# Half of wq's odd rows and all of gate_w moved to GpSimd's DMA queue in a decode kernel

## The chip, the cores and the metric

The kernel runs on one core of one Trainium2 chip. The metric is the device time of one execution in microseconds. Before the change it is 1295.29 us, the median of 3 runs (1294.97 to 1295.49).

## What is computed

A decode step for 8 sequences mixes two branches of the same input x of 8 x 576: attention over a cache of 4096 keys and values for each of 32 heads, and a layer-normed feed-forward block. A sigmoid gate, one number per sequence, weighs the two.

```python
B, Sq, D = 8, 1, 576
H, Sk, Dh = 32, 4096, 128            # all tensors bf16
q = (x @ wq)                         # 576 x 4096, one query per head
scores = einsum("bhqd,bhkd->bhqk", q, k_cache) * (Dh ** -0.5)
p = softmax(scores)
a = einsum("bhqk,bhkd->bhqd", p, v_cache) @ wo
h = gelu(einsum("bsd,df->bsf", layernorm(x), w1) + b1)
b = einsum("bsf,fd->bsd", h, w2) + b2
g = sigmoid((x * gate_w).sum(-1, keepdims=True))
out = g * a + (1 - g) * b
```

The two caches are 268 MB each; every byte of them is read once.

## The kernel before, in words

The work on the caches is cut into 32 groups `n`: one sequence and 8 heads each, with 8 MiB of K and 8 MiB of V. A group's K lies in `KR` with 128 partitions (8 heads x 16 stretches of the keys) and 256 keys of 128 numbers in each. VectorE multiplies K by the query in eight pieces (`mult`, L500), TensorE adds the products up in PSUM with an identity as weights (L511, L183), and VectorE reduces the rest (L523). Softmax follows on VectorE and ScalarE (`softmax`, L540 to L556), then the product with V on TensorE (`pv`, L564), whose result goes to `OT_sb`. After the last group TensorE multiplies `OT_sb` by wo (`a_proj`, L754).

The order of work is written out by hand, one list of operations per engine (`Stream.op`), and each engine runs its list in order. TensorE's and VectorE's lists are loops over the groups. Waits are on semaphores: an operation names those that it needs, a DMA has one of its own. An engine that waits holds up all that stands behind it in its list, DMA issues included.

Nearly all loads are issued by SyncE, in this order: wq, the first K tile in two halves, w1, w2 (`load_w2`, which waits for the Q projection because `VB` holds wq until then), the second K tile (`load_k`, L328, which waits until VectorE is through with the first), the first V tile in two parts (`load_v`, L339; the second part waits for the feed-forward block, whose w2 lies there), and then K and V in turn, each as soon as its buffer is free. After the last V tile come the pieces of wo. ScalarE issues four small loads at the start: x, gate_w (repeated for 8 partitions), b1 and b2. GpSimd issues no DMA before the change; it sets constants at the start and does some elementwise work.

The part that is changed is the start. wq has 576 rows of 4096. Rows 0 to 511 lie in `wq_sb`, four per partition, so that four matmuls of 128 rows each cover them. The other 64 rows, here called the odd rows, come as 128 half rows (`halves`, `wq_t`), one per partition. To match, `spread` writes the odd 64 columns of x twice into a zeroed tile `xz`, once at the even places and once at the odd ones, and `transposed` (L424) turns x and `xz` into `xT_sb`, with six columns blocks of 8. A matmul over all 128 partitions with block 4 then uses the first halves of the odd rows, one with block 5 the second halves. The Q projection (L451) is 40 matmuls: 2 halves of the heads, 4 groups, 5 blocks. ScalarE copies the result (L454), TensorE spreads it over partitions (`q_of`, L465), ScalarE copies it to `q_bc` (L469) and to `q_n` (L475), and VectorE's first product (L500) can start.

The gate's sum is one fused multiply and reduce on VectorE (`t_gs`, L407), its sigmoid one ScalarE activation with a table load (`a_g`, L410). The feed-forward block's transposes of the normalised x use the same `up_ps` bank from column `YT_COL` on.

Of the kernel before, what the change touches and what calls it, by code (L numbers as in the profile page):

```python
# [144 lines left out]
def bass_gated_mix__mha_block_cached__mixer_channel_mlp__decode_kernel(  # L145
# [71 lines left out]
    junk = early([B, D])  # L217
    xz = early([B, 2, 64, 2])
    yz = early([B, 2, 64, 2])
    xT_sb = early([128, NKF + 2, B])  # L220
    yT_sb = sb("yT_sb", [128, NKF + 2, B], BF16)
# [57 lines left out]
    up_bank = (qb_ps, *tr_ps)  # L279
    YT_COL = 64  # L280

# [4 lines left out]
    def load(engine, dst, src, name, waits=()):  # L286
        return op(engine, lambda e: e.dma_start(dst, src), waits, dma=(nc.alloc_semaphore(name), 16))  # L287
# [85 lines left out]
    c_mA = memset("gpsimd", mA[:], 0.0)  # L373
    c_shift = memset("gpsimd", shift[:], 0.0)
    zeros = bass.AP(tensor=mA, offset=1, ap=[[pstride(mA), 128], [0, 512]])

    def blank(ps):
# [28 lines left out]
                                                   op0=ALU.add), [t])  # L406
    t_gs = op("vector", lambda e: e.tensor_tensor_reduce(out=junk, in0=x_sb, in1=gw8, scale=1.0, scalar=0.0,  # L407
                                                         op0=ALU.mult, op1=ALU.add, accum_out=stat[:, 8:9]), [ld_gw, t1])
    a_sqrt = aside("scalar", lambda e: e.activation(out=stat[:, 5:6], in_=stat[:, 4:5], func=ACT.Sqrt), [t_vpe])
    a_g = aside("scalar", lambda e: e.activation(out=stat[:, 9:10], in_=stat[:, 8:9], func=ACT.Sigmoid), [t_gs])  # L410
    G_COL, OMG_COL = 9, 10


    def spread(dst, src, waits):

        aside("scalar", lambda e: e.activation(out=dst[:, 0, :, 0], in_=src[:, 512:576], func=ACT.Copy), [*waits, c_z])
        return aside("scalar", lambda e: e.activation(out=dst[:, 1, :, 1], in_=src[:, 512:576], func=ACT.Copy))

    def transposed(src, srcz, col, waits):
        last = None  # L420
        for kt in range(NKF + 2):
            o = up_ps[:, col + kt * B:col + (kt + 1) * B]
            i = src[:, kt:NKF * 128:NKF] if kt < NKF else srcz[:, kt - NKF, :, :].rearrange("b r s -> b (r s)")
# [4 lines left out]
    def untransposed(dst, col, waits):  # L428
        return op("vector", lambda e: e.tensor_copy(
            out=dst.rearrange("p k b -> p (k b)"), in_=up_ps[:, col:col + (NKF + 2) * B]), waits)  # L430

    v_xz = spread(xz, x_sb, [ld_x])
    p_xT = transposed(x_sb, xz, 0, [ld_x, c_id, v_xz])
    v_xT = untransposed(xT_sb, 0, [p_xT])
# [4 lines left out]
    p_yT = transposed(y_sb, yz, YT_COL, [v_yz, v_xT])  # L439
    v_yT = untransposed(yT_sb[:, :, :], YT_COL, [p_yT])  # L440

    a_Q = []
    p_Q = None
    for half in range(2):
        for h in range(4):
            for kt in range(NKT):
                o = tr_ps[half][32 * h:32 * h + B, :]
                at = (kt * SK + half * (SK // 2) if kt < NKF else NKF * SK) + h * DH
                r = bass.AP(tensor=VB, offset=at, ap=[[pstride(VB), 128], [4 * DH, 4], [1, DH]])
                xi = kt if kt < NKF else NKF + half  # L450
                p_Q = aside("tensor", lambda e, o=o, r=r, kt=kt, xi=xi: e.matmul(  # L451
                    o, lhsT=xT_sb[:, xi, :], rhs=r, start=(kt == 0), stop=(kt == NKT - 1)),
                    [v_xT, *ld_wq, *c_ps] if h == kt == half == 0 else ())
        a_Q.append(aside("scalar", lambda e, half=half: e.activation(  # L454
            out=Q4[:, half * 512:(half + 1) * 512], in_=tr_ps[half][:, :], func=ACT.Copy, scale=inv_sqrt_dh), [p_Q]))
# [443 lines left out]
```

## Time and profile before

| | |
|---|---|
| median of 3 runs | 1295.29 us (1294.97 to 1295.49) |
| profiled execution, span of its instructions | 1293.1 us |
| around the span, by the median | 2.2 us |
| busy: TensorE / VectorE / ScalarE / GpSimd | 731.3 / 851.9 / 73.2 / 12.7 us |
| read from memory | 556.95 MB |

The span runs from the first to the last instruction of the profiled execution, and no time of its own is given for that execution outside of it; the 2.2 us are the median of the three runs less the span. Times in the views are microseconds from the start of the span. PE is TensorE, PEld its weight loads, DVE VectorE, ACT ScalarE, POOL GpSimd, SP SyncE; a `q` behind a name is the engine's sequencer, which issues DMAs. `L451` is line 451 of the kernel before. In rows in order of time the columns are start, duration, engine, line, operation, output and input, count, and in brackets the idle time ahead of it with what ended it. In rows by window the columns are the stretch, its length, busy time and count of each engine, the granted TensorE clock, the busy share of the 16 DMA engines and GB/s. In rows on DMA issues the last number is the time from issue to landing; in rows on queues the numbers are packets, MB and the share of 16 DMA engines' time.

### The profile page before, as it was taken

Reading aid. Unit: us, or ns where it says so; the run is one execution under the profiler, and the core shown is the slowest. Engines: PE = TensorE matmul, PEld = TensorE weight load, DVE = VectorE, ACT = ScalarE, POOL = GpSimd, SP = SyncE. Lnnn points to the kernel's source line nnn. Section 1 sums busy time; section 2 is a strip of 40 time slices with the busy share of each in tenths; the row PEclk is TensorE's granted clock in tenths of the full one; section 3 lists DMA queues with packets and bytes.
Section 4 is the critical chain, followed back from the end, with each engine's and each line's share of the span. In section 5 each row is a group of like instructions: output and inputs, shape, how many; then the busy total and the mean of one; then the engine's idle time right before and its main releaser. Section 6 shows DMA issues by size and latency. Waiting matters only on the chain.

```text
span 1293.1 us, 10903 instructions
## 1 busy us (share of the span) xinstructions
PE 731.3 (57%) x4824; PEld 142.8 (11%) x3032; DVE 851.9 (66%) x1078; ACT 73.2 (6%) x164; POOL 12.7 (1%) x23
## 2 busy tenths in 40 slices
PE   3755566455556555556555556555556555557556
PEld 0211111011111011111011111001111001111003
DVE  3646667766667766667766667766668766667763
ACT  3300000000000000000000000000000000000001
POOL 0100000000000000000000000000000000000001
PEclk8978888877898787799778888877888877798878
DMA  9999999999999999999999999999999999999998
GB/s 405 427 447 424 430 442 430 438 432 430 442 428 428 444 426 430 444 428 438 434 428 442 428 428 444 428 428 444 428 438 434 428 442 428 428 444 428 428 438 356
DMA packets 11728, 557.07 MB, mean 431 GB/s; under 512 B 1448, under 2 KB 1608, under 8 KB 2120
## 3 DMA queue, kind: packets, MB, share of 16 engines
q1 hardware_dynamic: 11520, 556.93, 99.7%
q8 instruction: 5, 0.08, 0.0%
q10 hardware_dynamic: 200, 0.03, 0.0%
q14 instruction: 3, 0.02, 0.0%
HBM read 556.95 MB, written 0.01 MB: 431 GB/s over the span
## 4 chain that ended last, share of the span: by engine, by line
DMA 67%; DVE 18%; PE 9%; issue 5%; DVEq 1%; SPq 0%
DMA KR<-in_A_k_cache_dram 66%; DVE p L500 15%; PE psb L183 7%; DVE s_sb L523 2%; DMA KR<-in_A_wo_dram 2%; PE psb L511 2%; DVEq L523 0%; DVEq L137 0%; SPq L287 0%; PE psb L754 0%; DVE p L850 0%; DVEq L500 0%
## 5 line engine op out<-in xcount | busy, mean ns | idle before, releaser
L500 DVE TENSOR_TENSOR p<-KR,q_n 128x4096 bf16<-128x4096 bf16 x256 | 581.6, 2282 | 213.6 <-DMA KR<-in_A_k_cache_dram 213.6
L183 PE MATMUL psb<-p,ident 128*128 128x512 bf16 x1792 | 483.8, 415 | 0.0
L511 PE MATMUL psb<-p,ident 128*128 128x512 bf16 x256 | 112.1, 438 | 511.6 <-DVE p L500 511.6
L523 DVE TENSOR_REDUCE s_sb<-psb 128x512 f32 (+1 forms) x256 | 175.3, 685 | 106.9 <-PE psb L183 60.4
L511 PEld LDWEIGHTS psb<-p,ident 128*128 128x128 bf16 x256 | 26.1, 102 | 964.3 <-DVE p L500 963.8
L564 PE MATMUL psb<-VB,P 128*32 128x512 bf16 x1984 | 112.7, 380 | 0.0
L552 DVE TENSOR_SCALAR P<-E,own 128x256 bf16<-128x256 bf16 x256 | 53.1, 282 | 87.4 <-ACT E L549 87.4
L475 ACT ACTIVATE q_n<-q_bc 128x128 bf16<-128x128 bf16 x32 | 9.9, 310 | 871.3 <-DVE p L500 871.3
L564 PEld LDWEIGHTS psb<-VB,P 128*32 128x32 bf16 x1984 | 50.1, 97 | 47.9
L581 PE MATMUL psb<-selO,O_sb 128*128 128x8 f32 x256 | 33.9, 259 | 22.5 <-ACT O_sb L576 22.5
L581 PEld LDWEIGHTS psb<-selO,O_sb 128*128 128x128 f32 x256 | 31.0, 191 | 38.3 <-ACT O_sb L576 38.3
L576 ACT ACTIVATE O_sb<-psb 128x512 f32<-128x512 f32 x32 | 19.1, 597 | 197.9 <-PE psb L564 197.9
L571 PEld LDWEIGHTS psb<-rs,ones 128*128 128x128 f32 x64 | 12.1, 190 | 46.6 <-issue 44.4
L691 POOL TENSOR_TENSOR p<-OT_sb,fine 128x512 bf16<-128x512 bf16 (+1 forms) x4 | 5.0, 1278 | 1196.8 <-PE psb L571 1193.0
L549 ACT ACTIVATE E<-s_sb,mD 128x256 bf16<-128x256 f32 x32 | 16.0, 499 | 0.0
L540 DVE TENSOR_REDUCE mA<-s_sb 128x1 f32<-128x256 f32 x32 | 13.5, 420 | 1.1
L480 ACT ACTIVATE OT_sb<-O_n,G 128x8 bf16<-128x8 f32 x31 | 9.3, 301 | 84.3 <-DVE O_n L587 84.3
L555 DVE TENSOR_REDUCE es<-E 128x1 f32<-128x256 bf16 x32 | 13.2, 412 | 0.0
L571 PE MATMUL psb<-rs,ones 128*128 128x8 f32 x64 | 9.2, 216 | 1.3 <-DVE O_n L587 1.3
L653 PE MATMUL psb<-VB,hT_sb 128*8 128x288 bf16 x72 | 6.5, 358 | 4.7 <-POOL hT_sb L632 4.7
L556 DVE TENSOR_SCALAR rs<-own,es 128x8 f32<-128x8 f32 x32 | 7.4, 231 | 1.1
L548 DVE STREAM_TRANSPOSE mD<-mC 128x32 f32<-128x32 f32 x32 | 6.8, 212 | 1.1
(98 smaller groups left out, 125.8 us busy)
## 6 DMA issues: line engine op xcount, KB each, us to landing
KR<-in_A_k_cache_dram SPq DMA_DIRECT2D x2, 4096.0 KB, 27.2
VB<-in_A_v_cache_dram SPq DMA_DIRECT2D x1, 5376.0 KB, 27.1
VB<-in_B_w_dram SPq DMA_DIRECT2D x1, 5184.0 KB, 40.6
KR<-in_B_w_dram SPq DMA_DIRECT2D x1, 4608.0 KB, 43.2
VB<-in_A_wq_dram SPq DMA_DIRECT2D x1, 4096.0 KB, 12.5
KR<-in_A_v_cache_dram SPq DMA_DIRECT2D x1, 4096.0 KB, 22.3
VB<-in_A_v_cache_dram SPq DMA_DIRECT2D x1, 2816.0 KB, 38.4
KR<-in_A_wo_dram SPq DMA_DIRECT2D x1, 2304.0 KB, 20.7
```

The lines of the kernel that those rows point to most:

```text
L183: return e.add_instruction(mybir.InstMatmult(name=nc.get_next_instruction_name(), engine=mybir.EngineType.PE, ins=[e.lower_ap(rhs), e.lowe ...
L500: v_mult[n, c] = op("vector", lambda e: e.tensor_tensor(out=p1[:, par, :, :], in0=k_of(), in1=qb, op=ALU.mult), [k_land[n, s], a_q[n], p_s ...
L511: fn = lambda e, r=r: e.matmul(tr_ps[par][:, :], lhsT=ident[:, :], rhs=r, start=True, stop=False)
L523: v_red[n, c] = op("vector", lambda e: e.tensor_reduce(out=s_of(), in_=tr_ps[par][:, :].rearrange("p (t c) -> p t c", c=CH), axis=AX.X, op ...
L540: t = op("vector", lambda e: e.tensor_reduce(out=mA[:, 0:1], in_=s_sb[:, :], axis=AX.X, op=ALU.max), [v_red[n, NC - 1], c_mA])
L549: a_exp[n] = op("scalar", lambda e: e.activation(out=E[:, :], in_=s_sb[:, :], func=ACT.Exp, bias=mD[:, 0:1], scale=1.0), [v_nm[n], v_P.get ...
L552: v_P[n] = op("vector", lambda e, h=h: e.tensor_scalar(out=P[:, :, h, :], in0=E[:, :].rearrange("p (q t) -> p q t", t=TQ), scalar1=own[:, ...
L555: t = op("vector", lambda e: e.tensor_reduce(out=es[:, :], in_=E[:, :], axis=AX.X, op=ALU.add), [a_exp[n]])
L564: p_pv[n] = op("tensor", lambda e, o=o, tq=tq, at=at, v=v: e.matmul(o, lhsT=P[:, tq, :, :].rearrange("p h t -> p (h t)"), rhs=v.rearrange( ...
L571: p_z[n] = op("tensor", lambda e: e.matmul(oz_ps[:, HB:2 * HB], lhsT=ones[:, :], rhs=rs[:, :], start=True, stop=True), [v_rs[n], v_norm.ge ...
L576: a_ev[n] = op("scalar", lambda e: e.activation(out=O_sb[:].rearrange("p t d -> p (t d)"), in_=o_ps[n // last][:, :], func=ACT.Copy), [p_p ...
L581: p_oz[n] = op("tensor", lambda e, tt=tt: e.matmul(o, lhsT=O_sb[:, tt, :], rhs=selO[:, tt, :], start=(tt == 0), stop=(tt == TQ - 1 and stop)),
```

## The change

The 64 odd rows of wq are divided. Rows 512 to 543 come as 128 quarter rows of 2 KB, one per partition, still from SyncE. Rows 544 to 575 come whole, 8 KB each, to partitions 64 to 95 of `VB` behind the quarter rows, in four transfers of 8 rows from GpSimd: transfer `j` takes every fourth row from `j` on. Ahead of each of the four GpSimd loads a quarter of gate_w (144 numbers, repeated for 8 partitions); ScalarE's load of gate_w goes.

`spread_x` takes the place of `spread` for x: four copies of 32 columns for the quarter rows, and one at places 64 to 95 for the whole rows, so `xT_sb` has nine blocks instead of six. The Q projection has seven matmuls for each head group instead of five: four as before, two of 256 columns for two quarters each, and one over 32 partitions (`p0` to `p1_`) for the whole rows. The gate's reduction moves behind the transposes and waits for the four quarters. The rest is as before.

```diff
-    wq_t = view(VB, 4 * SK, [128, SK // 2])
+    XQ = 4
+    XR = 64 // 2
+    XP = 64
+    wq_t = view(VB, 4 * SK, [128, SK // XQ])
+    WQB = 4 * SK + SK // XQ
...
-    ld_gw = load("scalar", gw8, bcast(gate_w), "ld_gw")
...
-             load("sync", wq_t, halves(A_wq), "ld_wqb")]
+             load("sync", wq_t, A_wq[512:512 + XR, :].rearrange("r (s n) -> (r s) n", s=XQ), "ld_wqb")]
...
+    ld_gw = []
+    for j in range(4):
+        c0, n = j * D // 4, D // 4
+        ld_gw.append(load("gpsimd", gw8[:, c0:c0 + n],
+                          bass.AP(tensor=gate_w.tensor, offset=gate_w.offset + c0, ap=[[0, B], [1, n]]), f"ld_gw{j}"))
+        ld_wq.append(load("gpsimd",
+                          bass.AP(tensor=VB, offset=(XP + j) * pstride(VB) + WQB, ap=[[4 * pstride(VB), B], [1, SK]]),
+                          bass.AP(tensor=A_wq.tensor, offset=A_wq.offset + (512 + XR + j) * SK, ap=[[4 * SK, B], [1, SK]]),
+                          f"ld_wqc{j}"))
...
+    def spread_x(waits):
+
+        def into(at, ap):
+            return bass.AP(tensor=xz.tensor, offset=xz.offset + at, ap=[[pstride(p1), B]] + ap)
+
+        xr = x_sb[:, 512:512 + XR]
+        aside("scalar", lambda e: e.activation(
+            out=into(0, [[129, XQ], [XQ, XR]]),
+            in_=bass.AP(tensor=xr.tensor, offset=xr.offset, ap=[[pstride(p1), B], [0, XQ], [1, XR]]), func=ACT.Copy), [*waits, c_z])
+        return aside("scalar", lambda e: e.activation(out=into(XQ * 128 + XP, [[1, XR]]), in_=x_sb[:, 512 + XR:576], func=ACT.Copy))
...
-            for kt in range(NKT):
-                o = tr_ps[half][32 * h:32 * h + B, :]
-                at = (kt * SK + half * (SK // 2) if kt < NKF else NKF * SK) + h * DH
+            r0 = 32 * h
+            for kt in range(NKF + 3):
+                if kt < NKF:
+                    at, p0, p1_, g, o0, xi = kt * SK + half * (SK // 2), 0, 128, 4, 0, kt
+                elif kt < NKF + 2:
+                    at, p0, p1_, g, o0, xi = NKF * SK, 0, 128, 2, (kt - NKF) * 2 * DH, 2 * half + kt
+                else:
+                    at, p0, p1_, g, o0, xi = WQB + half * (SK // 2), XP, XP + XR, 4, 0, NKF + XQ
+                o = tr_ps[half][r0:r0 + B, o0:o0 + g * DH]
```

GpSimd's list at the start, before, from the last constants to the first work on the feed-forward block (`p` holds x and its spread copies):

```order
L365 MEMSET p 8x256 x2
L365 MEMSET ones 128x128
L365 MEMSET mA 128x32
L365 MEMSET shift 128x240
L794 TENSOR_SCALAR stat<-ident,stat 8x8
L626 TENSOR_TENSOR Q<-Q,b_sb 128x288
```

The same place after the change:

```order
L368 MEMSET shift 128x240
L291 DMA p<-in_gate_w_dram 8x144
L291 DMA VB<-in_A_wq_dram 8x4096
L291 DMA p<-in_gate_w_dram 8x144
L291 DMA VB<-in_A_wq_dram 8x4096
L291 DMA p<-in_gate_w_dram 8x144
L291 DMA VB<-in_A_wq_dram 8x4096
L291 DMA p<-in_gate_w_dram 8x144
L291 DMA VB<-in_A_wq_dram 8x4096
L823 TENSOR_SCALAR stat<-ident,stat 8x8
```

Eight DMA issues now stand between the last constant and the gate's diagonal.

VectorE's list before, from the end of the layer norm's statistics to the first product of K and q:

```order
L405 TENSOR_SCALAR stat<-stat 8x1
L407 ISA p,stat<-p 8x576
L407 ISA stat 8x1
L429 CAST p<-psb 128x48
L435 RECIPROCAL stat<-stat 8x1
L436 TENSOR_SCALAR p<-p,stat 8x576
L429 CAST yT_sb<-psb 128x48
L500 TENSOR_TENSOR p<-KR,q_n 128x4096 x2
```

The same place after the change:

```order
L417 TENSOR_SCALAR stat<-stat 8x1
L450 CAST p<-psb 128x72
L456 RECIPROCAL stat<-stat 8x1
L457 TENSOR_SCALAR p<-p,stat 8x576
L450 CAST yT_sb<-psb 128x48
L462 ISA p,stat<-p 8x576
L462 ISA stat 8x1
L529 TENSOR_TENSOR p<-KR,q_n 128x4096 x2
```

The gate's reduction (`ISA p,stat<-p 8x576`) has moved from ahead of the two transposes to just ahead of the first product.

More of the change, by code (lines that the diff above doesn't have):

```diff
@@ L217, in bass_gated_mix__mha_block_cached__mixer_channel_mlp__decode_kernel @@
     junk = early([B, D])
[L218 removed]
+    xz = early([B, XQ + 1, 128])
     yz = early([B, 2, 64, 2])
[L220 removed]
+    xT_sb = early([128, NKF + XQ + 1, B])
     yT_sb = sb("yT_sb", [128, NKF + 2, B], BF16)
@@ L426, in transposed, with untransposed @@
         return last
-    def untransposed(dst, col, waits):
+    def untransposed(dst, col, n, waits):
         return op("vector", lambda e: e.tensor_copy(
[L430 to L434, printed above, removed]
+            out=dst.rearrange("p k b -> p (k b)"), in_=up_ps[:, col:col + n * B]), waits)
+    v_xz = spread_x([ld_x])
+    p_xT = transposed(x_sb, [xz[:, i, :] for i in range(XQ + 1)], 0, [ld_x, c_id, v_xz])
+    v_xT = untransposed(xT_sb, 0, NKF + XQ + 1, [p_xT])
     t = op("vector", lambda e: e.reciprocal(out=stat[:, 7:8], in_=stat[:, 5:6]), [a_sqrt])
@@ L438, in bass_gated_mix__mha_block_cached__mixer_channel_mlp__decode_kernel @@
     v_yz = spread(yz, y_sb, [v_y])
-    p_yT = transposed(y_sb, yz, YT_COL, [v_yz, v_xT])
-    v_yT = untransposed(yT_sb[:, :, :], YT_COL, [p_yT])
+    p_yT = transposed(y_sb, [yz[:, i, :, :].rearrange("b r s -> b (r s)") for i in range(2)], YT_COL, [v_yz, v_xT])
+    v_yT = untransposed(yT_sb[:, :, :], YT_COL, NKF + 2, [p_yT])
+    t_gs = op("vector", lambda e: e.tensor_tensor_reduce(out=junk, in0=x_sb, in1=gw8, scale=1.0, scalar=0.0,
+                                                         op0=ALU.mult, op1=ALU.add, accum_out=stat[:, 8:9]), [*ld_gw, t1])
+    a_g = aside("scalar", lambda e: e.activation(out=stat[:, 9:10], in_=stat[:, 8:9], func=ACT.Sigmoid), [t_gs])
     a_Q = []
@@ L445, in bass_gated_mix__mha_block_cached__mixer_channel_mlp__decode_kernel @@
         for h in range(4):
-            for kt in range(NKT):
-                o = tr_ps[half][32 * h:32 * h + B, :]
-                at = (kt * SK + half * (SK // 2) if kt < NKF else NKF * SK) + h * DH
[L449 to L452, printed above, removed]
+            r0 = 32 * h
[7 more added lines that the diff above has]
+                o = tr_ps[half][r0:r0 + B, o0:o0 + g * DH]
+                r = bass.AP(tensor=VB, offset=p0 * pstride(VB) + at + h * DH, ap=[[pstride(VB), p1_ - p0], [4 * DH, g], [1, DH]])
+                p_Q = aside("tensor", lambda e, o=o, r=r, kt=kt, xi=xi, p0=p0, p1_=p1_: e.matmul(
+                    o, lhsT=xT_sb[p0:p1_, xi, :], rhs=r, start=(kt == 0), stop=(kt == NKF + 2)),
                     [v_xT, *ld_wq, *c_ps] if h == kt == half == 0 else ())
```

10 lines of the change are left out of this document (4 added, 6 removed).

## The prediction

> **What bounds the kernel now.** I read the page's head and its DMA table first, then the chain that ended last, then busy time by windows for the middle of the run, its start and its end, and at last the opening in order of time.
>
> ```profile
> span 1293.1 us, 10903 instructions
> DMA packets 11728, 557.07 MB, mean 431 GB/s; under 512 B 1448, under 2 KB 1608, under 8 KB 2120
> q1 hardware_dynamic: 11520, 556.93, 99.7%
> q8 instruction: 5, 0.08, 0.0%
> q10 hardware_dynamic: 200, 0.03, 0.0%
> DMA 67%; DVE 18%; PE 9%; issue 5%; DVEq 1%; SPq 0%
> ```
>
> One queue, q1 (SyncE's), moves 556.93 of 557.07 MB and keeps the 16 DMA engines 99.7% busy over the whole span. The chain names DMA for 67%; the rest of it (VectorE, TensorE) is time in which the chain passes through the consumers of a K tile, while the DMA engines go on with a V tile. That the engines do not pause is to be seen in the windows:
>
> ```profile
> core 0: us, PE busy (x) PEld busy (x) DVE busy (x) ACT busy (x) POOL busy (x), PEclk, DMA share, GB/s
> 0.00:8.00 8.00, 0.00 (x0) 0.00 (x0) 2.78 (x10) 5.39 (x9) 1.64 (x11) 1.00 0.85 330
> 1288.00:1288.50 0.50, 0.50 (x24) 0.50 (x20) 0.00 (x0) 0.00 (x0) 0.00 (x0) 0.50 0.93 360
> 1288.50:1289.00 0.50, 0.48 (x18) 0.17 (x8) 0.00 (x0) 0.00 (x0) 0.00 (x0) 0.50 0.53 203
> 1289.00:1289.50 0.50, 0.03 (x4) 0.03 (x8) 0.00 (x0) 0.00 (x0) 0.00 (x0) 0.50 0.34 131
> 1289.50:1290.00 0.50, 0.50 (x20) 0.44 (x20) 0.00 (x0) 0.00 (x0) 0.00 (x0) 0.50 0.27 97
> 1290.00:1290.50 0.50, 0.50 (x20) 0.12 (x8) 0.00 (x0) 0.00 (x0) 0.00 (x0) 0.50 0.01 2
> 118.25:157.00 38.75, 21.25 (x138) 3.78 (x82) 26.41 (x34) 1.60 (x4) 0.00 (x0) 0.85 1.01 436
> ```
>
> In one turn of the loop (118.25 to 157.00) the DMA share is 1.01, at 436 GB/s. So the time is bytes divided by the pace of the DMA engines, plus the start, plus the tail, and a change at the start counts in two ways only: if it empties SyncE's queue, or if it changes what each single DMA engine has to carry. The last rows show that the second one exists. The engines do not finish together: 0.53 of 16 are busy in 1288.5 to 1289.0, 0.34 (5.4 engines) in the next half microsecond, 0.27 (4.3 engines) in the one after, 0.01 after 1290. The end waits for the last of about five late engines, which run 1 to 1.5 us behind the bulk. The row q8 has five instruction fetches of 0.08 MB together, 16 KB each; five fetches on five engines would fit five late ones, though no view shows which engine carried what.
>
> **The change, part by part.** First, whether SyncE's queue can run empty. The opening, in order of time:
>
> ```profile
> 0.75 0.59 ACTq L287 DMA_DIRECT2D p<-in_A_x_dram  x1
> 1.36 0.28 ACTq L287 DMA_DIRECT2D p<-in_gate_w_dram  x1
> 2.12 0.29 POOL L365 MEMSET shift<- 128x240 bf16 x1
> 2.81 0.74 DVE L397 TENSOR_REDUCE stat<-p 8x1 f32<-8x576 bf16 x1
> 2.86 0.48 SPq L287 DMA_DIRECT2D KR<-in_B_w_dram  x1
> 7.76 1.28 ACT L410 ACT_TABLE_LOAD   x1
> 8.04 0.75 DVE L407 CUSTOM_DVE_ANT_0 p<-p 8x576 bf16<-8x576 bf16 x1 [3.21 <-DMA p<-in_gate_w_dram]
> 9.06 0.20 ACT L410 ACTIVATE stat<-stat 8x1 f32<-8x1 f32 x1
> 14.71 4.45 PE L451 MATMUL psb<-VB,p 128*8 128x512 bf16 x40 [3.06 <-DMA VB<-in_A_wq_dram]
> 19.18 0.33 SPq L287 DMA_DIRECT2D VB<-in_B_w_dram  x1
> 20.91 0.31 ACT L475 ACTIVATE q_n<-q_bc 128x128 bf16<-128x128 bf16 x1
> 24.30 4.49 DVE L500 TENSOR_TENSOR p<-KR,q_n 128x4096 bf16<-128x4096 bf16 x2 [12.41 <-DMA KR<-in_A_k_cache_dram]
> 47.20 0.33 SPq L328 DMA_DIRECT2D KR<-in_A_k_cache_dram  x1
> 47.57 0.44 SPq L339 DMA_DIRECT2D VB<-in_A_v_cache_dram  x1
> 63.51 1.41 POOL L632 TENSOR_TENSOR hT_sb<-Q 128x288 bf16<-128x288 f32 x1 [0.55 <-ACT Q L631]
> 71.58 0.33 SPq L339 DMA_DIRECT2D VB<-in_A_v_cache_dram  x1
> VB<-in_B_w_dram SPq DMA_DIRECT2D x1, 5184.0 KB, 40.6
> KR<-in_B_w_dram SPq DMA_DIRECT2D x1, 4608.0 KB, 43.2
> VB<-in_A_v_cache_dram SPq DMA_DIRECT2D x1, 2816.0 KB, 38.4
> b_sb<-in_B_b_dram ACTq DMA_DIRECT2D x1, 9.0 KB, 12.0
> ```
>
> The Q projection (L451) starts at 14.71, when wq is in; q_n is ready at 20.91 + 0.31 = 21.22; the first product of K and q starts only at 24.30, since it waits for K. That is a cover of 3.1 us. A second cover lies behind it. When the products of this first K tile are through, SyncE issues the next K load, at 47.20. What stands ahead of it in the queue is w2, issued at 19.18 and landed 40.6 later, at 59.8. A load at the free start (x, issued at 0.75) was read by VectorE 2.1 us later, at 2.81, so the engines run dry only if that issue slips past about 57.7: by 10.5 us.
>
> GpSimd now issues eight DMAs, after its last memset (2.12 + 0.29 = 2.41). The trace has no DMA from GpSimd, so I bound it. Below: eight at the 0.28 of ScalarE's issue of gate_w, 2.2 us, and the 6.7 from that issue (1.36) to the reader's start (8.04): landed at 11.3, ahead of the rest of wq, which PE had at 14.71 anyhow. Above: eight at 1.41, the longest single GpSimd instruction in the trace, 11.3 us, and 12.0 to landing as for b1: 25.7. I take 18, the middle, since no row is nearer to either end. The Q projection then runs 56 matmuls instead of 40: 40 of 512 columns as before (eight of them now over 32 partitions) and 16 new ones of 256, so 24,576 columns in place of 20,480. By columns 4.45 becomes 5.3 us, by instructions 6.2. From its end (19.16) to the end of q_n it was 2.06. With wq in at T, the product starts at T + 8.3 at most: in time for 24.30 up to T = 16.0, and in time for the DMA queue up to T = 26.5. At T = 18 VectorE starts its first product 1.1 to 2 us later; even at 25.7 it is 34.0, that is 9.7 later, under the 10.5. Two more issues wait for the same work. w2's goes out at 19.18 and would go out by 32, while w1 ahead of it lands at 2.86 + 43.2 = 46.1. The second V load goes out at 71.58, after the feed-forward block; the V load ahead of it lands at 47.57 + 38.4 = 86.0, which leaves 12.3 us. **Cost on the end: 0 from both bounds.**
>
> The wait that is added: the gate's reduction (0.75 on VectorE) now stands ahead of the first product and waits for all four quarters of gate_w; behind it on VectorE is the product, which waits for wq's last rows, issued later, in any case. The gate's sigmoid (a table load of 1.28 and 0.20) stands ahead of the copies of Q on ScalarE, within 2.3 us of gate_w; the Q projection's first half takes more. Both hidden, as are the three more transposes of x.
>
> Second, the bytes. They are the same. There are 56 packets more (128 rows of 4 KB and 8 of gate_w become 128, 32 and 32). q10's 200 small packets took under 0.05% of 16 engines' span, so under 52 ns each: 56 of these on 16 engines are under 0.2 us; I take 0.
>
> Third, which engine carries them, and here a term is left. Row q10 says how a transfer of 8 rows is dealt out. ScalarE's and the output's small transfers have 156 rows (x 8, gate_w 8, b1 128, b2 4, output 8), and 44 more packets are left of 200: 8 + 8 + 16 + 4 + 8, one per engine used, if a transfer of 8 rows uses 8 engines and one of 128 all 16. So each of GpSimd's four transfers of wq should put one 8 KB row on each of 8 engines. If the four take the same 8, these carry 32 KB each, where an even spread of the 256 KB would be 16 KB. At 431/16 = 26.9 GB/s per engine, 16,384 B are 0.61 us: **half of the engines finish 0.61 us later, the other half 0.61 earlier**. Bounds: 0 if they alternate; if a transfer sits on a single engine, more, below.
>
> [...]
>
> The end is set by the latest engine, so the sign depends on where the five late ones sit. If all five sat in the relieved half, the end would come 0.61 earlier; placed at random, that has 56 chances in 4368, 1.3%. With one of the latest among the loaded, it comes 0.61 later. PE waits for the last pieces of wo at the end, so it passes through:
>
> ```profile
> 1289.47 1.36 PE L754 MATMUL psb<-KR,OT_sb 128*8 128x144 bf16 x32 [0.49 <-DMA KR<-in_A_wo_dram]
> ```
>
> **Sum:** queue 0, packets 0, balance +0.6: span 1293.1 + 0.6 = 1293.7. Around the span there are 1295.29 - 1293.1 = 2.2 us, against the median of the runs, and nothing in the change adds there: 1295.9.
>
> **The rivals.**
>
> Late engines in the relieved half. Five fetches need not be placed at random; some order by which they are dealt out could hold all of them in one half. Nothing in the views speaks against it. Time: 1295.3 - 0.6 = 1294.7.
>
> The change doesn't do what it says to the engines: the four transfers alternate or spread over 16. Time: 1295.3.
>
> A transfer on fewer engines: 64 KB on one engine, four times on four engines. Each then carries 64 - 16 = 48 KB more, 1.8 us: 1297.1. On one and the same engine it would be 240 KB, 8.9 us: 1304. The count of q10 speaks against it, for ScalarE's queue.
>
> GpSimd is slow enough that the queue runs dry: slower than before. The place is GpSimd's issue of eight DMAs, the point T = 26.5 for wq's last rows. If each issue also waits out a VectorE instruction of 0.75 (the longest ahead of the first product), eight at 2.16 end at 19.7, and with 12.0 to landing T is 31.7: 5.2 us past the point, all idle: 1300.5. Against it: VectorE is busy for only 2.78 of the first 8 us and idle for 12.41 ahead of the first product (both rows above), so few issues would meet it.
>
> [...]
>
> Faster by more than 0.2% would need 2.6 us. All that the DMA engines lose is 0.15 of the first 8 us, 1.2, and the uneven end, about 1; no part of the change returns most of both.
>
> **How the numbers follow.** The forecast (+0.6) has 0.50; late engines relieved (1294.7) 0.27; evenly spread (1295.3) 0.13; fewer engines (1297.1 or 1304) 0.04; queue dry (1300.5) 0.05; faster by over 0.2% 0.01. 0.2% is 2.6 us, about what a measurement of this kernel can tell from no change. So faster 0.01; same 0.50 + 0.27 + 0.13 + 0.02 = 0.92 (with the half of the fewer-engines case that costs 1.8); slower 0.07. The range reaches from the relieved case, less 0.4 for runs that differ (1294.97 to 1295.49 before) and a placing in between, to the 1.8 of the fewer-engines case: 1294.3 to 1297.1.
>
> **What would show it.** In the DMA table a new queue with GpSimd's rows, 0.27 MB. In the opening, the Q projection starting between 14.7 and 25.7, the first product at 24.3 to 34.0, the second K load issued before 57.7, and a DMA share of 1.0 in 47 to 65; a share that falls there is the dry queue. At the end, shares by half microseconds: a longer tail, some engines busy until 1290.6, means the loaded half held a late engine; a shorter one, ending about 1289.4, the relieved half; the same shape, even spreading. A shift of 2 us or more with a full DMA share and the old tail would prove me wrong altogether: then something outside these steps counts, such as time before the first load.

## The result and the profile after

| | before | after |
|---|---|---|
| median of 21 runs each, side by side | 1295.19 us (1294.76 to 1296.22) | 1296.84 us (1296.36 to 1298.2) |
| span of the profiled execution | 1293.1 us | 1294.8 us |
| ratio after / before | | 1.0014, 95% interval 1.0007 to 1.002 |

The change costs 1.65 us. The forecast was +0.6 in a range of -1.0 to +1.8 around 1295.3, so the sign and the range held, and the size did not: two thirds of the loss are not in the sum.

A landing, in what follows, is a record in the trace of the end of a part of a transfer. K's first half has 16 of them (in the kernel before from 23.71 to 24.28 us); the profile counts 16 DMA engines, so I read them as one per engine, though no record names one. A median of single kernels below carries an interval of about 1.2 us to either side by its ratio, so small differences between medians are not read alone, but together with the spread of the runs and the traces.

The head of the page after the change, its DMA table and its chain:

```profile
span 1294.8 us, 10952 instructions
DMA packets 11968, 557.08 MB, mean 430 GB/s; under 512 B 1664, under 2 KB 1816, under 8 KB 2328
q1 hardware_dynamic: 11520, 556.67, 99.6%
q0 software_dynamic: 256, 0.27, 0.1%
DMA 64%; DVE 18%; PE 11%; issue 5%; DVEq 1%; POOL 1%; ACT 0%; SPq 0%; POOLq 0%
```

The new queue q0 is GpSimd's, with the 0.27 MB that the change moves there. SyncE's queue is as busy as before, and the bytes are the same to 0.01 MB: what changed is the pace, 430 instead of 431 GB/s.

The opening after the change, in order of time:

```profile
2.71 0.75 POOL L291 DMA_DIRECT2D p<-in_gate_w_dram  x1
6.53 0.52 POOL L291 DMA_DIRECT2D VB<-in_A_wq_dram  x1
15.96 0.75 DVE L462 CUSTOM_DVE_ANT_0 p<-p 8x576 bf16<-8x576 bf16 x1 [5.80 <-DMA p<-in_gate_w_dram]
17.52 14.81 PE L480 MATMUL psb<-VB,p 128*8 128x512 bf16 x56 [7.60 <-DMA VB<-in_A_wq_dram]
32.36 0.33 SPq L291 DMA_DIRECT2D VB<-in_B_w_dram  x1
34.49 4.49 DVE L529 TENSOR_TENSOR p<-KR,q_n 128x4096 bf16<-128x4096 bf16 x2 [17.77 <-ACT q_n L504]
56.80 0.33 SPq L331 DMA_DIRECT2D KR<-in_A_k_cache_dram  x1
```

and its DMA issues, with the time from issue to landing in the last column:

```profile
KR<-in_A_k_cache_dram SPq DMA_DIRECT2D x2, 4096.0 KB, 28.8
VB<-in_A_wq_dram POOLq DMA_DIRECT2D x4, 64.0 KB, 10.2
p<-in_gate_w_dram POOLq DMA_DIRECT2D x4, 2.2 KB, 9.9
```

GpSimd is through with its eight issues at 7.05, and wq is complete at 17.5 (forecast: 18). The Q projection then takes 14.81 us, where I had 5.3 to 6.2. So the first product starts at 34.49 instead of 24.30, and K's second load is issued at 56.80 instead of 47.20, 0.9 ahead of the point (57.7) at which I had the queue run dry. Whether this long projection is where the time went is a question for the experiments.

The pace of the DMA engines while wq's odd rows and the first K tile land, in the same 12 us of the kernel before and of the one after:

```profile
12.00:24.00 12.00, 4.85 (x42) 2.04 (x42) 0.00 (x0) 2.10 (x4) 0.00 (x0) 1.00 1.03 437
```

```profile
12.00:24.00 12.00, 6.48 (x17) 1.70 (x18) 0.76 (x2) 0.20 (x1) 0.31 (x1) 1.00 0.98 381
```

The last two numbers are the DMA share and GB/s. The engines are almost as busy (0.98 and 1.03) but move 381 instead of 437 GB/s: 56 GB/s less for 12 us is 0.67 MB, which at 437 GB/s takes 1.54 us. Nearly the whole loss is in this stretch, long before 56.80. Engines that are about as busy and move less should be waiting inside their packets; the records of single packets, further down, show that they do.

The end after the change, by half microseconds:

```profile
1288.00:1288.50 0.50, 0.12 (x3) 0.13 (x4) 0.32 (x1) 0.00 (x0) 0.00 (x0) 0.50 0.93 380
1288.50:1289.00 0.50, 0.49 (x8) 0.33 (x7) 0.00 (x0) 0.00 (x0) 0.00 (x0) 0.50 0.95 366
1289.00:1289.50 0.50, 0.00 (x0) 0.00 (x0) 0.43 (x1) 0.00 (x0) 0.00 (x0) 0.50 0.91 350
1289.50:1290.00 0.50, 0.49 (x20) 0.49 (x24) 0.00 (x0) 0.00 (x0) 0.00 (x0) 0.50 0.70 277
1290.00:1290.50 0.50, 0.50 (x24) 0.34 (x12) 0.00 (x0) 0.00 (x0) 0.00 (x0) 0.50 0.54 207
1290.50:1291.00 0.50, 0.16 (x8) 0.00 (x0) 0.00 (x0) 0.00 (x0) 0.00 (x0) 0.50 0.37 136
1291.00:1291.50 0.50, 0.37 (x16) 0.37 (x20) 0.00 (x0) 0.00 (x0) 0.00 (x0) 0.50 0.17 62
1291.50:1292.00 0.50, 0.50 (x24) 0.23 (x12) 0.00 (x0) 0.00 (x0) 0.00 (x0) 0.50 0.05 16
```

The tail is longer and also wider. The eight shares add up to 4.62 half microseconds, the five of before to 2.08: the average engine ends 1.27 us later. A mere shift of load from one half of the engines to the other, which was my term, would have left the average where it was. So the engines lost time on average, and were not only loaded unevenly.

### The profile page after: what moved, and what is told of

It reads as the page before. It is cut to its first block, busy times and chain, and to the rows that moved or that the text cites. A ratio compares the mean times of both kernels' runs of the same rounds, so it can differ in the third digit from the quotient of the medians.

```text
span 1294.8 us, 10952 instructions
## 1 busy us (share of the span) xinstructions
PE 745.9 (58%) x4843; PEld 145.6 (11%) x3051; DVE 851.9 (66%) x1078; ACT 73.3 (6%) x164; POOL 19.5 (2%) x31
## 4 chain that ended last, share of the span: by engine, by line
DMA 64%; DVE 18%; PE 11%; issue 5%; DVEq 1%; POOL 1%; ACT 0%; SPq 0%; POOLq 0%
DMA KR<-in_A_k_cache_dram 61%; DVE p L529 16%; PE psb L183 7%; DVE s_sb L552 2%; DMA KR<-in_A_wo_dram 2%; PE psb L540 1%; PE psb L480 1%; DMA VB<-in_A_wq_dram 1%; PE psb L682 0%; DVEq L552 0%; PE psb L643 0%; DVEq L137 0%; PE psb L634 0%; POOL p L291 0%; SPq L291 0%
## 5 line engine op out<-in xcount | busy, mean ns | idle before, releaser
L480 PE MATMUL psb<-VB,p 128*8 128x512 bf16 (+2 forms) x56 | 14.8, 408 | 7.6 <-DMA VB<-in_A_wq_dram 7.6
```

The costliest lines, as they stand in the source:

```text
L480: p_Q = aside("tensor", lambda e, o=o, r=r, kt=kt, xi=xi, p0=p0, p1_=p1_: e.matmul(o, lhsT=xT_sb[p0:p1_, xi, :], rhs=r, start=(kt == 0), s ...
```

## The experiments

Twelve kernels, each beside the kernel before on the same chip. The kernel before had 1295.03 to 1295.06 us there. The code shows only the lines of an edit on which its point rests; `...` stands for the rest.

### Many GpSimd transfers beside the old wq

The first suspect was GpSimd itself, since after the change its eight transfers are what is new in the slow stretch. This kernel has before's load of wq and its Q projection, and gate_w in 16 pieces from GpSimd:

```diff
-    ld_gw = load("scalar", gw8, bcast(gate_w), "ld_gw")
+    for j in range(16):
+        c0, n = j * D // 16, D // 16
+        ld_gw.append(load("gpsimd", gw8[:, c0:c0 + n],
+                          bass.AP(tensor=gate_w.tensor, offset=gate_w.offset + c0, ap=[[0, B], [1, n]]), f"ld_gw{j}"))
...
```

> The kernel before, with wq loaded and used as it was; gate_w alone comes from GpSimd, in 16 pieces of 36 numbers instead of one load from ScalarE, and the gate's reduction stands just ahead of the first product as in the changed kernel. Theory S (every DMA from GpSimd costs each of the 16 DMA engines a fixed 0.15 us while SyncE's loads run, so eight of them make the uniform 1.2 us that the changed kernel lost): 16 x 0.15 = 2.4 us slower than before, 1297.6 against 1295.2, with all engines late alike. Theory R (the loss comes from the small rows of wq, 2 KB and 8 KB, between the 32 KB ones): no change, within 0.2 us, since wq is loaded as before and 9 KB of gate_w are nothing.

Measured: 1300.17 us (1299.82 to 1300.47), ratio 1.0039 (1.0026 to 1.0053), which neither of the two theories had. The pace from 12 to 24:

```profile
12.00:24.00 12.00, 5.45 (x40) 2.21 (x40) 0.00 (x0) 0.00 (x0) 0.00 (x0) 0.98 1.04 435
```

435 GB/s against 437: these 16 small transfers from GpSimd did not slow the stream. The 5 us come from elsewhere:

```profile
34.20 0.75 DVE L443 CUSTOM_DVE_ANT_0 p<-p 8x576 bf16<-8x576 bf16 x1 [24.23 <-DMA p<-in_gate_w_dram]
38.06 4.49 DVE L505 TENSOR_TENSOR p<-KR,q_n 128x4096 bf16<-128x4096 bf16 x2 [3.11 <-issue]
60.95 0.33 SPq L327 DMA_DIRECT2D KR<-in_A_k_cache_dram  x1
```

The gate's reduction waits for the last of the 16 pieces until 34.20. The gate's sigmoid and, behind it on ScalarE, the copies of Q wait for the reduction, so the first product starts at 38.06, and K's second load goes out at 60.95. The DMA engines then have nothing to do, in a window by itself; the three rows are this kernel, the kernel before and the change:

```profile
57.00:66.00 9.00, 7.20 (x54) 1.68 (x41) 6.43 (x10) 2.25 (x5) 0.00 (x0) 1.00 0.63 238
57.00:66.00 9.00, 4.08 (x30) 3.33 (x31) 2.00 (x10) 2.13 (x3) 3.97 (x5) 0.60 1.08 464
57.00:66.00 9.00, 8.33 (x75) 4.52 (x68) 2.30 (x8) 3.96 (x7) 0.00 (x0) 1.00 0.97 408
```

A share of 0.63 over 9 us leaves 3.3 us empty here, and against the 464 GB/s of the kernel before 2.0 MB are missing, 4.7 of the 5.1 us. This is the rival in which the queue runs dry, at a price near the one I had given it (1300.5), with the wait for gate_w in place of slow issues. The change as it is shows no such gap: 0.97.

### The rows without GpSimd

Here gate_w is with ScalarE again, and the 32 whole rows come in one transfer of 32 from SyncE, to partitions 64 to 95 as in the change:

```diff
+             load("sync", bass.AP(tensor=VB, offset=XP * pstride(VB) + WQB, ap=[[pstride(VB), XR], [1, SK]]),
+                  A_wq[512 + XR:576, :], "ld_wqc")]
...
```

> The changed kernel without any DMA from GpSimd: the 32 whole rows come in one transfer of 32 rows from SyncE behind the quarter rows, gate_w in one load from ScalarE. Small rows and the 56 matmuls of the Q projection stay; with 32 rows all 16 DMA engines should carry two rows each, so nothing is unbalanced. Theory S: no uniform loss and no imbalance, 1295.2 to 1295.4, equal to before. Theory R: the uniform 1.2 us stays, 1296.4. The Q projection tells a third thing: if its 14.8 us in the changed kernel come from its form, it takes about 14 us here too; if from GpSimd's transfers, 5 to 6.

Measured: 1296.17 us (1295.61 to 1296.88), ratio 1.0007 (0.9998 to 1.0016).

```profile
12.00:24.00 12.00, 7.14 (x26) 2.25 (x27) 0.00 (x0) 0.00 (x0) 0.00 (x0) 1.00 1.03 391
```

With no transfer from GpSimd at all the pace is 391 GB/s at a share of 1.03. Two thirds of the loss, 1.1 us, belong to the rows and not to the queue that issues them. The profiled execution is the longest of the eleven (1296.88), so 391 may be a little low for this kernel; the same rows in one transfer from GpSimd, further down, have 394 in an execution of 1296.11.

### The transfers of eight rows, with and without GpSimd

Two kernels cut the 32 rows into four transfers of eight again: one from GpSimd without the quarters of gate_w between them, one from SyncE.

```diff
+    ld_gw = [load("scalar", gw8, bcast(gate_w), "ld_gw")]
...
-        ld_gw.append(load("gpsimd", gw8[:, c0:c0 + n],
-                          bass.AP(tensor=gate_w.tensor, offset=gate_w.offset + c0, ap=[[0, B], [1, n]]), f"ld_gw{j}"))
```

> The changed kernel with gate_w in one load from ScalarE again; GpSimd issues the four transfers of wq alone. Theory S with the balance term: four DMAs from GpSimd cost 4 x 0.15 = 0.6 us on all engines; without a gate_w load between them the transfers should alternate between the two halves of the DMA engines, so the 0.6 us of imbalance goes: 1295.8 against 1295.2 before and 1296.8 for the changed kernel. Theory R: 1.2 us stay and the imbalance goes, 1296.4. If the transfers of wq do not alternate, 0.5 more in either case, and the engines' ends lie in two groups 1.2 us apart.

```diff
+             *(load("sync", bass.AP(tensor=VB, offset=(XP + j) * pstride(VB) + WQB, ap=[[4 * pstride(VB), B], [1, SK]]),
+                    bass.AP(tensor=A_wq.tensor, offset=A_wq.offset + (512 + XR + j) * SK, ap=[[4 * SK, B], [1, SK]]),
+                    f"ld_wqc{j}") for j in range(4))]
...
```

> The changed kernel without any DMA from GpSimd, but with the four transfers of 8 rows kept, issued by SyncE behind the quarter rows; gate_w in one load from ScalarE. This is the imbalance alone, if a transfer of 8 rows from SyncE uses the same 8 DMA engines each time. Theory S with the balance term: no uniform loss, 0.5 to 0.6 us later at the end because at least one of the late engines is in the loaded half, 1295.7 to 1295.8. Theory R: 1.2 us more than that, 1296.9. If imbalance did nothing: 1295.2.

Measured: 1296.94 us (1296.75 to 1298.08), ratio 1.0014 (1.0005 to 1.0023), and 1296.9 us (1296.33 to 1297.49), ratio 1.0013 (1.0004 to 1.0022). Both are the change over again, so neither the queue nor the quarters matter. Against the one transfer of 32 rows, cutting costs 0.7 to 0.8 us more. The trace's records of landings say why. When K's first half lands, the 16 engines of the kernel before finish in one group, from 23.71 to 24.28. In the one with eight rows from SyncE eight finish at 24.37 to 24.87 and eight at 25.60 to 26.07, in the change at 24.40 to 24.74 and 25.58 to 25.89: two groups 1.2 us apart, which is 32 KB at 26.9 GB/s. That fits all four transfers sitting on the same eight engines, as the forecast assumed.

That such transfers from GpSimd alternate between two halves of the engines once no quarter of gate_w stands between them, as expected for the first of these kernels, is shown by no run: without the quarters the landings are in the two groups as well, and the time is 1296.94.

### Where the rows are put

What is left is 1.1 us that 32 rows in 32 partitions cost and 128 half rows in 128 partitions do not. Two differences are open: the pieces (2 KB and 8 KB for 4 KB) and the destination (partitions 64 to 95 for all 128). The first kernel moves the 32 rows to every fourth partition, the second brings all odd rows as quarter rows. Both, and the later kernels with spread rows, leave out the product with 32 of the rows, so their Q projection is shorter; three kernels below show that this is not what saves the time (two without that product still lose 1.0 and 1.7 us, and one with a short projection and that product loses 1.8).

```diff
-             load("sync", bass.AP(tensor=VB, offset=XP * pstride(VB) + WQB, ap=[[pstride(VB), XR], [1, SK]]),
+             load("sync", bass.AP(tensor=VB, offset=WQB, ap=[[4 * pstride(VB), XR], [1, SK]]),
...
```

> The run with 32 whole rows from SyncE again (1296.17 us, all transfers balanced, 1.1 us above before), with one thing changed: the 32 rows go to every fourth of the 128 partitions instead of to the 32 partitions 64 to 95. The product with these rows is left out, so the attention's Q is short of 32 inputs. Theory P (a transfer into 32 neighbouring partitions lands at a lower rate, and that is most of the lost 1.1 us): the stage of these rows falls from 1.44 us towards the 0.6 us of its bytes, K0 lands some 0.8 us earlier, and the time falls to 1295.2 to 1295.6. Theory L (any row longer or shorter than before's costs it, or the 32 descriptors do, wherever they go): time stays at 1295.9 to 1296.4. Without the 32-row matmuls among the 128-row ones, the Q projection should also say why it took 14 us: if these matmuls did it, it falls to some 5.3 us, and if the 256-column ones did it, it stays near 12.

```diff
+             load("sync", view(VB, WQB, [128, SK // XQ]), A_wq[512 + XR:576, :].rearrange("r (s n) -> (r s) n", s=XQ), "ld_wqc")]
...
```

> All 64 odd rows as quarter rows: two transfers from SyncE of 128 pieces of 2 KB into all 128 partitions, no transfer into 32 partitions, balanced. The product with the second 32 rows is left out. Theory Q (pieces of 2 KB cost 0.06 us each more than their bytes: 8 of them took 1.08 us on an engine instead of 0.6): 16 on each engine lose 0.9 to 1.0 us, and the time is 1295.9 to 1296.2. Theory P (the 32 neighbouring partitions are what costs, quarter rows little): 1295.0 to 1295.4.

Measured: 1295.1 us (1294.78 to 1295.24), ratio 1.0 (0.9991 to 1.0009), and 1295.18 us (1295.03 to 1295.42), ratio 1.0001 (0.9992 to 1.001). The pace with the spread rows:

```profile
12.00:24.00 12.00, 6.27 (x50) 2.44 (x50) 0.00 (x0) 2.10 (x4) 0.00 (x0) 1.00 1.03 437
```

437 GB/s, as before. The slowest of the 11 runs with spread rows took 1295.24 us, the fastest of the 11 with the rows in 64 to 95 1295.61. Here the pieces cost nothing, long or short; the destination cost it all. The third kernel puts all 64 odd rows into partitions 0 to 63, with one matmul over 64 rows for them:

```diff
-    wq_t = view(VB, 4 * SK, [128, SK // XQ])
+    wq_t = bass.AP(tensor=VB, offset=4 * SK, ap=[[pstride(VB), 64], [1, SK]])
...
+             load("sync", wq_t, A_wq[512:576, :], "ld_wqb")]
...
```

> All 64 odd rows whole, in one transfer from SyncE into partitions 0 to 63 (64 pieces of 8 KB instead of 128 of 4 KB, balanced, four on each engine), and one 64-row matmul for them. Theory P (neighbouring partitions, fewer than all, take a transfer at a lower rate; 32 of them took 256 KB in 1.44 us): half of the partitions take 512 KB in some 2.4 us instead of 1.2 to 1.34, and the time is 1295.9 to 1296.3. Theory L (the count and size of the pieces is what matters): 64 pieces instead of 128 cost no more than before, and the time is 1294.8 to 1295.2.

Measured: 1296.58 us (1296.3 to 1296.82), ratio 1.0011 (1.0002 to 1.002).

```profile
12.00:24.00 12.00, 7.73 (x25) 1.90 (x25) 0.00 (x0) 0.60 (x1) 0.00 (x0) 1.00 1.04 394
```

Half of the partitions, twice the rows, half as many pieces as before: 394 GB/s and 1.5 us lost, somewhat more than expected. The records of single packets agree: an 8 KB row took 0.31 us on its engine when the rows were spread (0.34 at most), 0.57 in the middle and up to 0.85 in partitions 64 to 95, and 0.60 in the middle here. The engine is counted as busy with it all the while: the share in 12 to 24 was 1.03 with the rows in 64 to 95 and 1.04 here.

Packets of the stream beside these rows are slow too. Of those of 32 KB that start between 11 and 18 us, all 80 took 1.21 to 1.24 us in the kernel before and 1.21 to 1.22 with the rows spread; in the change 24 of 65 took over 1.25, up to 1.90. The time that packets from 9 to 24 us took beyond the usual for their size (1.213 us for 32 KB, 0.309 for 8 KB, 0.084 for 2 KB) is 1.22 us per engine in the change, 1.45 here and 0.02 with the rows spread. By so much the average engine is late with K's first half: by 1.25, 1.46 and 0.06 us.

The fourth asks what about the destination it is. The rows go to every second partition of 64 to 127, side by side with none:

```diff
-             load("sync", bass.AP(tensor=VB, offset=WQB, ap=[[4 * pstride(VB), XR], [1, SK]]),
+             load("sync", bass.AP(tensor=VB, offset=XP * pstride(VB) + WQB, ap=[[2 * pstride(VB), XR], [1, SK]]),
...
```

> The run with the spread 32 rows from SyncE (1295.1 us), at every second partition of 64 to 127 instead of every fourth of 0 to 127; the product with these rows is left out. 64 whole rows in partitions 0 to 63 took some 2.7 us instead of 1.2, so 64 neighbouring partitions take about 197 GB/s. If the rate belongs to the range of partitions, 256 KB take 1.3 us instead of 0.6 and the time is 1295.6 to 1295.9 us, between the 1295.1 of the full range and the 1296.17 of 64 to 95. If only partitions side by side are slow, a gap of one heals it: 1294.9 to 1295.3. If the upper half of the partitions is slow as such: 1296.0 to 1296.4.

Measured: 1296.0 us (1295.86 to 1296.32), ratio 1.0008 (0.9999 to 1.0017).

```profile
12.00:24.00 12.00, 6.76 (x50) 2.60 (x50) 0.00 (x0) 2.10 (x4) 0.00 (x0) 1.00 1.00 396
```

396 GB/s. A gap of one heals nothing, and doubling the range from 32 to 64 partitions heals little: 1.0 us instead of 1.1. My case of a rate that belongs to the range missed by 0.1 us only, with runs from 1295.86 on, so the time alone does not refute it; the pace, as low as in 64 to 95, speaks against it. The case of the upper half as such held, though partitions 0 to 63 are slow as well.

The paces above fall into two classes: 391, 396 and 394 GB/s with the rows in 64 to 95, in every second of 64 to 127 and in 0 to 63, and 437 with the rows in every fourth of 0 to 127. What sets the first three apart from the last is not shown. If the rows are dealt out evenly, two per engine for 256 KB and four for 512 KB, an estimate of the loss from the row times is 2 x (0.57 - 0.31) = 0.5 us and 4 x (0.60 - 0.31) = 1.2 us; the runs show 1.1 and 1.5. The longest rows (up to 0.85 us in 64 to 95) and the slow 32 KB packets of the stream are not in this estimate and may make up the difference.

### Both terms in the change itself

Three kernels go back to GpSimd's queue: the four transfers with each row 16 partitions from the next, one transfer of 32 rows to 64 to 95, and one of 32 rows to every fourth partition.

```diff
-                          bass.AP(tensor=VB, offset=(XP + j) * pstride(VB) + WQB, ap=[[4 * pstride(VB), B], [1, SK]]),
+                          bass.AP(tensor=VB, offset=4 * j * pstride(VB) + WQB, ap=[[16 * pstride(VB), B], [1, SK]]),
...
```

> The change as it is, with GpSimd's four transfers of eight rows going to every sixteenth of the 128 partitions (together every fourth) instead of to neighbouring ones within 64 to 95; the product with these 32 rows is left out. The theory has two terms: 1.1 us for the destination in 32 neighbouring partitions, which should go, and some 0.7 us because each transfer of eight rows is carried by the same eight of the 16 DMA engines, which should stay: 1295.6 to 1295.9 us, with the landings of K0 still in two groups of eight engines 1.2 us apart. Rival: the two groups are themselves an effect of the destination, and nothing is left: 1294.9 to 1295.3.

```diff
+        if j == 3:
+            ld_wq.append(load("gpsimd", bass.AP(tensor=VB, offset=XP * pstride(VB) + WQB, ap=[[pstride(VB), XR], [1, SK]]),
+                              A_wq[512 + XR:576, :], "ld_wqc"))
```

> The change with its four transfers of eight rows from GpSimd joined into one of 32 rows, behind the last quarter of gate_w; destination in partitions 64 to 95 as in the change. If the imbalance comes from the eight pieces of a transfer (a transfer of 32 pieces gives two to each of the 16 engines), only the cost of the destination stays: 1296.0 to 1296.4 us, as the same rows from SyncE (1296.17). Rival: transfers from GpSimd's queue are carried by eight engines whatever their count of pieces: 1296.7 to 1297.1.

```diff
+            ld_wq.append(load("gpsimd", bass.AP(tensor=VB, offset=0 + WQB, ap=[[4 * pstride(VB), XR], [1, SK]]),
...
```

> Both at once: one transfer of 32 rows from GpSimd, to every fourth of the 128 partitions, the product with these rows left out. If the two terms are all that the change costs, this is the kernel before again: 1294.9 to 1295.3 us. If GpSimd's queue costs something of its own that the other terms hid: 1295.4 or more.

Measured, in this order: 1296.7 us (1296.48 to 1296.94), ratio 1.0012 (1.0003 to 1.0021); 1296.02 us (1295.76 to 1296.25), ratio 1.0007 (0.9998 to 1.0016); 1295.26 us (1294.95 to 1295.42), ratio 1.0001 (0.9992 to 1.001). The pace of the three, in the same order:

```profile
12.00:24.00 12.00, 6.51 (x47) 2.65 (x48) 0.75 (x2) 0.80 (x2) 0.31 (x1) 1.00 1.01 383
```

```profile
12.00:24.00 12.00, 8.08 (x30) 2.47 (x31) 0.76 (x2) 0.32 (x2) 0.31 (x1) 1.00 1.01 394
```

```profile
12.00:24.00 12.00, 6.68 (x50) 2.60 (x50) 0.76 (x2) 2.30 (x5) 0.31 (x1) 1.00 1.02 435
```

The last two came out as forecast. One transfer in place of four takes away 0.65 us (1.65 to 1.0 above before), and a destination in every fourth partition the remaining 1.0 but for 0.2. So GpSimd's queue may carry these rows at next to no cost.

The first is a miss: 383 GB/s and 1296.7, no better than the change, where I expected 1295.6 to 1295.9. By the landings its engines finish K's first half in one group again (25.37 to 25.85), all of them late. My edit had not taken away the cost of the destination, as I meant it to. A transfer's rows go to partitions 4j, 4j + 16, 4j + 32 and so on, and the packets show that this destination is even slower than that of the change: the last 16 of its 32 rows took 0.67 us in the middle where those of the change took 0.48, and all its packets together lost 1.57 us per engine where those of the change lost 1.22. Why it is slower is not shown, and no further run was made for it. It stays open why its engines end in one group, the sign of my rival there: 32 KB on eight of them should still set these 1.2 us behind, unless the others lost as much or the rows were dealt out otherwise. It also means that transfers of eight rows were never measured with a destination that costs nothing.

### The long Q projection

The change as it is, with the four 32-row matmuls of each half behind its 24 others:

```diff
-        for h in range(4):
-            r0 = 32 * h
-            for kt in range(NKF + 3):
+        for ks in (range(NKF + 2), range(NKF + 2, NKF + 3)):
+            for h, kt in ((h, kt) for h in range(4) for kt in ks):
+                r0 = 32 * h
```

> The change as it is, with the matmuls of the Q projection in another order: for each half of the columns first the 24 matmuls over 128 rows, then the four over 32 rows, where the change has one of these behind each six. If the alternation is what keeps the four column groups from running beside each other, the projection falls from 14.8 us to 5.5 to 8 us, the first product starts some 7 to 9 us earlier (near 26 us) and K1's load is issued near 48 us instead of 56.8. If the queue of SyncE ran dry at 56.8 us and this cost time, the kernel's time falls by that: to 1296.0 to 1296.5; if it cost nothing, the time stays at 1296.7 to 1297.0. If the projection keeps its 14 us, the other suspects are the 256-column matmuls.

Measured: 1296.88 us (1296.58 to 1298.04), ratio 1.0015 (1.0006 to 1.0024).

```profile
17.81 7.58 PE L480 MATMUL psb<-VB,p 128*8 128x512 bf16 x56 [7.91 <-DMA VB<-in_A_wq_dram]
25.43 0.33 SPq L291 DMA_DIRECT2D VB<-in_B_w_dram  x1
50.78 0.33 SPq L331 DMA_DIRECT2D KR<-in_A_k_cache_dram  x1
```

The same 56 matmuls take 7.58 us instead of 14.81 (13.65 in the kernel with 32 rows from SyncE, so GpSimd's transfers don't make it long), and K's second load goes out at 50.78 instead of 56.80. The time does not move. The long projection was the most striking thing in the trace after the change, and it costs nothing: the queue holds out until then (in the change a DMA share of 0.97 from 57 to 66, where the kernel whose queue ran dry has 0.63). Without the 32-row matmuls at all (the kernel with the spread rows) the 48 others take less still:

```profile
14.64 5.86 PE L474 MATMUL psb<-VB,p 128*8 128x512 bf16 x48 [4.34 <-DMA VB<-in_A_wq_dram]
```

So it is the change between matmuls over 128 rows and over fewer, eight times in the change, that lengthens the projection. The records of single matmuls show how: in the kernel before four start close together (15.86, 15.87, 15.90 and 15.94), in the change one starts after the other (17.52, 17.90, 18.33 and 18.75). Why the one form keeps the others apart is not shown.

No kernel here beats the one before; the best, with both costs removed, come back to it.

## Why the prediction was right or wrong

**What bounds the kernel: right.** Bytes over the pace of the DMA engines decide, and a delay at the start is carried to the end unchanged: by the trace's landings the last engine is 1.6 us behind that of before when K's first half lands (25.89 against 24.28), and 1.7 us behind when the fourth K tile does (158.45 against 156.74), and so it stays to the end.

**The queue, 0: right, with two wrong sizes.** wq in at 17.5 was forecast as 18. The projection was sized by columns (5.3) or by instructions (6.2) and took 14.81, since I took the pace of 4.45 us for 40 matmuls over to a row of mixed shapes; with the wait for wq this used up 9.6 us (56.80 against 47.20) of the 10.5 of cover. The point at which the queue runs dry was late as well: with an issue at 60.95 the kernel with 16 pieces lost 5.1 us, so the point is near 55.9, not 57.7. I had taken the landing of w2's last engine (59.80), and the other 15 finish at 58.03 to 58.61. In the change the stream itself is later, which gave some of it back; the reordered projection shows that nothing was lost there.

**Packets, 0: right as far as it went, and here is the step that failed.** "Second, the bytes. They are the same." I priced the number of packets and nothing else, and that is indeed 0 (the kernel with 256 quarter rows), though the table shows 240 more of them and not 56. What I did not price is where the packets go. 256 KB of whole rows went to partitions 64 to 95, and with them there the pace from 12 to 24 was 391 to 394 GB/s instead of 435 to 437: 1.0 to 1.1 us by the runs, the largest term of all. The diff names these partitions (`XP = 64`), and the prediction uses the number 32 only to count matmul rows.

**Balance, +0.6: the size held, the mechanism only in part.** That the four transfers take the same eight engines was my estimate; no run shows it, since no record names an engine, and what the runs showed in its place are two groups of eight landings. Four transfers of eight measure 0.65 (GpSimd, four against one) to 0.75 (SyncE), with the two groups 1.2 us apart that 32 KB make. But the term was to hold up one half of the engines and relieve the other, and no half was relieved. By the landings of the fourth K tile the average engine is 1.07 us behind that of before with one transfer and 1.40 with four, the last engine 1.04 and 1.71: half of these 0.67 is a delay of all engines, and only the other half is unevenness. Whether one of the latest engines was among the loaded ones isn't shown either.

**Sum.** Destination 1.0, balance 0.65, queue and packets 0: 1.65, as measured. The two terms come from pairs of runs and overlap, as the missed run of the spread eights and the landings show; some 0.3 us of the split is uncertain. That the time lay in the range is luck: the forecast lacked the largest term and was 1.05 us short of the measured difference, and the range reached up to 1297.1 for the sake of transfers on fewer engines, which didn't happen.

**The rivals.** Late engines relieved, evenly spread and fewer engines are excluded by the landings. (In the last of these, 240 KB on one engine are 9.1 us by the prediction's pace, not 8.9.) The dry queue exists at 1300.2, but takes twice as many GpSimd transfers as the change has. GpSimd's issues did not wait out instructions of VectorE, which would have made 2.16 us of each: the eight took 0.52 to 0.75 us each.

**What would prove me wrong.** I named a shift of 2 us with a full DMA share as the sign of something outside my steps. The sign was right and the threshold too high: 1.65 us with a share of 0.98, and a pace of 381 GB/s beside it, was that something.

## What to carry to other kernels

When a load is reshaped, ask which partitions it lands in, not only how many bytes and packets it has: here, beside a stream that kept the engines busy, an 8 KB row took 0.57 us in 32 neighbouring partitions and 0.60 in 64, and 0.31 in every fourth of 128 in one transfer. The 32 neighbours cost 1.1 us, every second of one half 1.0, and every fourth of 128 nothing (1295.1 us). Then ask how many rows one transfer has: four transfers of eight rows to 64 to 95 left the engines in two groups 1.2 us apart, and what was lost at the start (the last engine 1.6 us behind) stayed until the end (1.7 us of span). A DMA share near 1 did not mean full pace: it was 1.03 at 391 GB/s and at 437. So read GB/s beside it, in the stretch that the change touches, before following the most striking stall.

## What was not expected of the hardware

- Eight 32-row matmuls among 48 others lengthen the Q projection from 5.86 to 14.81 us; behind the others, in two groups of four, to 7.58. With one 64-row matmul behind every four it took 11.7 us for 40.
- GpSimd issued 16 DMAs in 8.44 us, 0.53 each, but its later transfers land late beside a full stream: the last of 16 small pieces, issued by 10.8, was read at 34.20.
- Rows to partitions 64 to 95 or 0 to 63 took longer inside their packets: 0.31 us for an 8 KB row in every fourth partition became 0.57 and 0.60, and the DMA share, 1.03 and 1.04, counts all of it as busy.
